# The first unit of a linear-attention and MLP kernel in two halves of 128 tokens

## The chip, the cores and the metric

The kernel runs on 1 core of one Trainium2 chip. The metric is the device time of one execution in microseconds (us), as a median over executions.

The engines are named as in the profile: PE (TensorE, products), PEld (its weight loads), DVE (VectorE), ACT (ScalarE), POOL (GpSimd), SP (SyncE, which issues nearly all transfers). "L445" is line 445 of the kernel.

## The reference

A gated linear attention with a state of 48x48 per head, then an MLP over all 8 heads of a token.

```python
batch, n_heads, seq, head_dim = (4, 8, 768, 48)      # q, k, v, f_logit: float32
...
f = 1.0 / (1.0 + np.exp(-f_logit))
for t in range(S):
    state = f[:, :, t, :, None] * state + np.einsum('bhd,bhe->bhde', k[:, :, t], v[:, :, t])
    y[:, :, t] = np.einsum('bhd,bhde->bhe', q[:, :, t], state)
...
x = np.ascontiguousarray(attn_out.transpose(0, 2, 1, 3)).reshape(B * S, H * D)   # 3072 x 384
h = x @ w_in                                          # 384 x 2048
g = h * (1.0 / (1.0 + np.exp(-1.702 * h)))
return (g @ w_out).astype(np.float32)                 # 2048 x 384
```

The two weights of the MLP are float64, so the kernel also turns 2 x 6.3 MB of 8-byte words into float32.

## The kernel before

**Units.** The 3072 tokens are 12 units of 256, three to a batch entry. In a unit the tokens are two sets of 128, "f = 1" (the first 128, in order) and "f = 0" (the last 128, stored in reverse), each of two chunks of 64. Heads stand in pairs: 128 partitions are two heads of 64 rows, and a tile `X[:, s]` of 128x512 holds one set of q or k for the four pairs.

**Attention of a unit.** `turn` transposes f_logit, k and q by products with the identity (units 0 and 1, L376) and ScalarE writes them to `F` and `X` (L381); later units use VectorE's transposes (L364). `begin_gates` multiplies the gates in pairs, in quarters, and so on (GpSimd, L436). Then six levels, m = 1, 2, 4, 8, 16, 32: `set_aside` copies the keys to `Kc` (ScalarE, L514), `score` makes 16 products (L445), `promote` multiplies keys and queries by the gates of the level (VectorE, L539 for units 0 and 1, one instruction for keys and one for queries, both sets in each), and `evacuate` moves the masked scores to `A` (VectorE L486 and L505, for the last level ScalarE L495). `turn_k` turns the keys back (L618, L619, tile `kn`), the "S" part makes the chunks' sums (L666) and states (L688 to L692) and the products of `A` with v (`add`, L555), and the "W" part adds the products of the queries with the states (L713), copies y to `yT` (L728) and brings it into the MLP's layout `xT` by transfers (`to_x`, L778 and L783): head pairs of 2x48 rows become tiles of 128 rows.

**MLP.** Units 0 and 1 run it plainly: `mlp_h` (L1127, three products per 128 columns of w_in, then GELU by ScalarE, L1131) and `mlp_o` (L1141, one product of 384 columns per 128 rows of w_out and 128 tokens), in four blocks of four 128-wide pieces, whose results are summed (L1191, L1193). Unit 2 uses plain h products and a form of `mlp_o` with fewer products on sums of parts of w_out (L808, L894); units from 3 on also a form of `mlp_h` on sums of parts of w_in (L1033).

**Weights.** They come in 16 pairs, four to a block: two of w_in (ff 0 and 1, ff 2 and 3), then two of w_out. `fetch_weights` issues a pair (768 KB) on SP's queue into one of three buffers `bits`, so pair n can be issued when pair n - 3 is converted. The conversion is an activation on the high words in place (ScalarE, L239), low words times 2^-29 (VectorE, L235), high words shifted (VectorE, L228) and the sum into the weight (VectorE, L238).

**What sets the order.** For TensorE and GpSimd the program's order holds throughout; until `fill_order.close()` (L1383) it holds for all engines. `opening` writes out unit 0 by hand and puts unit 1's transposes between its levels. From unit 1 on, `follow` runs the parts of a unit and, behind each part, a string of steps from `PLAN`: "f" emits the next piece of MLP work from the list `fill` (four or three products), "c" one step of a conversion, "w" a fetch, "p" the beginning of a conversion, "s" a sum of weights, "k" a product that nobody uses (`keep_up`, L116). `HOLES` holds such steps for inside unit 2's levels. The list `fill` has blocks (unit, block) in the order (0,0), (0,1), then (1,0) with (1,1), (0,2) with (1,2), (0,3) with (1,3). An assertion keeps a product behind the conversion of its weights. PSUM for products comes from four banks in turn (`bank`).

Of the kernel before, what the change touches and what calls it, by code (L numbers as in the profile page):

```python
# [23 lines left out]
def kernel(  # L24
# [77 lines left out]
    chosen = []  # L102

    def bank(shape, name, lane=None):

        if lane is None:
            lane = chosen.pop(0) if chosen else next(turns) % 4
        return ps.tile(shape, F32, tag=f"mm{lane}", name=name, bufs=1)
# [11 lines left out]
    nc.scalar.activation(ones, ones, AF.Sigmoid)  # L120
# [22 lines left out]
    nc.gpsimd.memset(by_half[:, :, 1, :, R4 * D - 32:], 0.0)  # L143
# [30 lines left out]
    NGR = NFF // FG  # L174

# [15 lines left out]
    R_BY_ACT = range(0)  # L191
# [18 lines left out]
    def begin_pair(m):  # L210
# [19 lines left out]
        def low():  # L230
            t["r"] = tmp("a", 2).bitcast(I32)
            if m in R_BY_ACT:
                nc.scalar.activation(t["r"], lo.bitcast(U32), AF.Copy, scale=2.0 ** -29)
            else:
                ve.tensor_scalar(t["r"], lo.bitcast(U32), 2.0 ** -29, None, op0=ALU.mult)  # L235
# [4 lines left out]
        if m in R_BY_ACT:  # L240
            low()
        else:
            todo.append(low)
        todo.extend((high, both, None))

    def begin_next():

        if state["begin"] < len(pairs):
            begin_pair(state["begin"])
            state["begin"] += 1  # L250
# [12 lines left out]
    HOLES = {(N_FILL, 0): "ccp", (N_FILL, 1): "cwcc", (N_FILL, 2): "cwp", (N_FILL, 3): "cc", (N_FILL, 4): "cw"}  # L263
# [5 lines left out]
    def load_raw(n, j, engines=(nc.sync,)):  # L269
# [8 lines left out]
        if n < N_FILL:  # L278
            for a in range(NP):
                engine = engines[a * len(engines) // NP]  # L280
                to = by_pair[j][32 * a:32 * (a + 1), :, :R * D]
                if first < 0 and a == 0:

                    for r, rows in ((1, 16), (17, 15)):
                        engine.dma_start(
                            out=to[r:r + rows], in_=span(0, r * R - 1, [[R * D, rows], [S * D, 2], [1, R * D]])
                        )
                    engine.dma_start(out=to[:1, :, D:], in_=span(0, 0, [[R * D, 1], [S * D, 2], [1, (R - 1) * D]]))
                else:
                    engine.dma_start(out=to, in_=span(2 * a, first, [[R * D, 32], [S * D, 2], [1, R * D]]))  # L290
            return
# [46 lines left out]
    def attention(n):  # L338
# [19 lines left out]
        def turn(j, outs, fn=None, pieces=None):  # L358
# [12 lines left out]
            for j0 in pieces or range(0, R, 4):  # L371
# [7 lines left out]
                for f in (1, 0):  # L379
                    at, step = (j0, 1) if f else (HALF - 1 - j0, -1)  # L380
                    nc.scalar.activation(  # L381
                        view(outs(f), at, [[HALF, NP], [R * step, 16], [step, 4]]),
                        pt.rearrange("p j (a f i) -> p f a i j", a=NP, f=2)[:, 1 - f],
                        (AF.Tanh if n > 1 else AF.Sigmoid) if fn else AF.Copy, scale=0.5 if fn and n > 1 else 1.0,
                    )
            if fn and n > 1:
                half_up()
# [264 lines left out]

        @part("S")
# [134 lines left out]
        return (begin_f, begin, begin_k, begin_gates), parts, (open_level, open_evacuate, turn_k), lambda: reverse_v(n)  # L788
# [315 lines left out]
    xTs, halves = {}, []  # L1104

# [7 lines left out]
    def mlp_h(n, ffs, g):  # L1113
        t = {}

        def one(ff, c):
            if c == 0:
                if ff % FG == 0:

                    if not halves:  # L1120
                        new = g_tile(f"g_{n}_{ff}")
                        halves.extend((new[:, :FG], new[:, FG:]))
                        g["tile", ff // HF] = new
                    g[ff // FG] = halves.pop(0)
                t["ph"] = bank([P, U], f"h_{n}_{ff}")
            ph = t["ph"]
            nc.tensor.matmul(  # L1127
                ph, lhsT=w_in[:, ff // 2, c, ff % 2 * P:(ff % 2 + 1) * P], rhs=xTs[n][:, c, :], start=(c == 0), stop=(c == NK - 1)
            )
            if c == NK - 1:  # L1130
                nc.scalar.activation(g[ff // FG][:, ff % FG, :], ph, AF.Gelu_apprx_sigmoid)  # L1131
        return [(NK * U, lambda ff=ff: [one(ff, c) for c in range(NK)], ff // FG * NPC + ff % FG + 1) for ff in ffs]

    def mlp_o(n, ffs, g, done):
# [3 lines left out]
        def one(tt, ff):  # L1138
            if ff == ffs[0]:
                t["po"] = bank([P, DM], f"o_{n}_{tt}_{ff}")  # L1140
# [4 lines left out]
            if ff == ffs[-1]:  # L1145
                done(tt, t["po"])
        return [(DM, lambda tt=tt, ff=ff: one(tt, ff), ff // FG * NPC + FG + 2 + ff % FG // 2 * 2) for tt in range(U // P) for ff in ffs]
# [34 lines left out]
    def mlp_block(n, r):  # L1182
# [13 lines left out]
        return mlp_h(n, ffs, g), mlp_o(n, ffs, g, done)  # L1196
# [10 lines left out]
    def parts_of(n):  # L1207
# [3 lines left out]
        if n and n != N_FILL:  # L1211
            kind, scores = parts[0]
            _, ahead = units[n - 1][1][-1]
# [60 lines left out]
    def follow_steps(steps):  # L1274

        for step in steps:
# [5 lines left out]
            elif step == "p":  # L1282
                begin_next()
            elif step == "w":
                fetch_weights()
# [25 lines left out]
    def opening():  # L1311

        begin_f, begin, begin_k, begin_gates = units[0][0]
        next_f, next_q, next_k, next_gates = units[1][0]
        level, evacuate, turn_k = units[0][2]
        load_raw(0, 0)
        load_raw(0, 2)
        load_raw(0, 1, (nc.scalar,))
        fetch_weights()
        begin_f()  # L1320
        begin_gates()
        begin_k()
        begin()
        load_raw(1, 0)
        load_raw(1, 2)
        load_v(0)
        load_raw(1, 1)
        fetch_weights()
        fetch_weights()
        for l in range(NL):  # L1330
            chosen[:] = [2, 3][l % 2:][:1]
            level(l)
            if l in (2, 3):
                next_f((0, 4)[l - 2:][:1])
            elif l < NL - 1:
                keep_up(1)
            if l == 1:
                begin_pair(0)
                state["begin"] = 1

        nc.scalar.activation(q_end, q_end, AF.Gelu_apprx_sigmoid)
        chosen[:] = [2, 3]
        turn_k(0)
        turn_k(2)
        for l in range(NL - 1):
            evacuate(l)
            if l == 1:
                units[0][3]()
        chosen[:] = [2, 3, 2, 3]
        next_q()  # L1350
        begin_pair(1)
        state["begin"] = 2
        evacuate(NL - 1)
        units[0][1][-2][1]()
        next_gates()
        for _ in range(NOP):
            convert()
        fetch_weights()

    fill = []  # L1360
    opening()
    FIRST = 'k'
    PLAN = {
        3: (
            "fffffffsffsf", "fsffsffsf", "f", "fsfsfsffsfsfsf", "", "ffff", "ff", "ffffffffffffffffsffsf", "fffsf",
        ),
        1: (
            "cccwcccwkkkkk", "kkkcf", "cfccwf", "fcffcwffcffcf", "ffcc", "f", "cwc", "fcc", "ffcf", "pw", "fw", "ff",
            "fffffff",
        ),  # L1370
        2: (
            "ffff", "ffffffff", "fcfcfcwffcfcfcwfffcfcfcff", "sss", "fcfcfcfffffss", "fcfcfcffffffff", "",
            "fffffffffff",
# [3 lines left out]
    fill += mlp_blocks((1, 0), (1, 1)) + mlp_blocks((0, 2), (1, 2)) + mlp_blocks((0, 3), (1, 3))  # L1377
# [4 lines left out]
    assert state["fetch"] == len(pairs)  # L1382
    fill_order.close()  # L1383
    assert state["done"] == 2 * len(pairs) or moe_w_in.dtype == F32
# [49 lines left out]
```

## Time and profile before

| | us |
|---|---|
| median of 3 executions (586.05 to 587.43) | 586.17 |
| the profiled execution, its time | 587.35 |
| its span | 585.4 |
| busy in the span: PE, PEld, DVE, ACT, POOL | 564.4, 514.6, 441.0, 288.8, 142.5 |
| first product of the MLP (L1127) starts | 38.95 |
| first product of unit 1's MLP starts | 69.36 |

TensorE is the busiest engine. A busy TensorE isn't one at its peak, since the ends of products are modelled; the weight loads beside it and the idle products (L116: four at the start and 24 between 13.3 and 38.7 us) tell more. A matrix product in float32 shows as two instructions. The time of an engine's wait matters only where what it then does ends last.

### The profile page before, as it was taken

The page shows a single profiled execution, that of the slowest core. Times are in us where ns is not written, and L with a number is a line of the kernel's source. Part 1 is how long each engine was busy: PE and PEld are TensorE (multiplying, and loading weights), DVE is VectorE, ACT ScalarE, POOL GpSimd, SP SyncE. Part 2 cuts the span into 40 slices and gives each one's busy share as a digit, 9 for nine tenths or more (in the row PEclk, how much of TensorE's full clock was granted, in tenths as well). Part 3 has the DMA queues.
Part 4 walks back from the last instruction along what each step waited for, and adds up shares of the span by engine and source line. Part 5 has one row for each costly group of instructions (what it writes and reads, how often), then busy time and mean ns, then how long its engine had stood idle before and what let it go on. Part 6 is the DMA issues. An engine that isn't in the chain of part 4 may idle for free.

```text
span 585.4 us, 18532 instructions
## 1 busy us (share of the span) xinstructions
PE 564.4 (96%) x7838; PEld 514.6 (88%) x7838; DVE 441.0 (75%) x697; ACT 288.8 (49%) x588; POOL 142.5 (24%) x226
## 2 busy tenths in 40 slices
PE   7899889999999999999999999999999999999997
PEld 6767667676899999999999999999999999999896
DVE  2898877986888786887796897786897786461284
ACT  4755354323543563564563564563563563652440
POOL 4020220614452602402502502502402403103000
PEclk9999999999999999999999999999999999999999
DMA  7869695833352452453542343442451211001000
GB/s 183 197 185 221 172 241 133 234 79 89 100 143 55 126 125 58 116 128 82 131 113 56 103 128 86 126 115 57 120 130 43 64 39 29 29 2 36 19 1 28
DMA packets 86771, 60.34 MB, mean 103 GB/s; under 512 B 33505, under 2 KB 78465, under 8 KB 86689
## 3 DMA queue, kind: packets, MB, share of 16 engines
q1 hardware_dynamic: 86208, 58.57, 40.0%
q8 instruction: 62, 1.02, 0.7%
q10 hardware_dynamic: 481, 0.59, 0.4%
q14 instruction: 20, 0.16, 0.1%
HBM read 45.49 MB, written 8.91 MB: 93 GB/s over the span
## 4 chain that ended last, share of the span: by engine, by line
PE 73%; DVE 10%; DMA 7%; SPq 4%; ACT 3%; issue 2%; ACTq 0%; DVEq 0%
PE h L1033 17%; PE o_Y L894 14%; PE o_Z L894 9%; PE h_y L1033 6%; PE sc L445 6%; PE o_X L894 5%; PE o_W L894 4%; DMA bits<-in_moe_w_in_dram 3%; PE h L1127 3%; PE o L1141 3%; DVE X L364 2%; PE y L713 2%; PE y L555 2%; PE sc L666 2%; DVE X L543 1%
## 5 line engine op out<-in xcount | busy, mean ns | idle before, releaser
L543 DVE TENSOR_TENSOR X<-X,tot 128x1024 f32<-128x1024 f32 x50 | 67.7, 1354 | 44.7 <-PE sc L445 38.4
L514 ACT COPY Kc<-X 128x512 f32<-128x512 f32 x72 | 48.4, 672 | 81.6 <-DVE X L543 61.2
L995 POOL TENSOR_TENSOR E<-xT 128x128 f32<-128x128 f32 (+1 forms) x36 | 16.0, 455 | 229.4 <-DMA xT<-yT 229.4
L1127 PE MATMUL h<-xT,w_in 128*128 128x256 f32 x288 | 65.9, 383 | 2.6 <-DMA xT<-yT 1.8
L1127 PEld LDWEIGHTS h<-xT,w_in 128*128 128x128 f32 x288 | 53.7, 190 | 12.3 <-issue 2.4
L1033 PE MATMUL h<-E,w_in 128*128 128x128 f32 (+1 forms) x476 | 62.8, 277 | 0.5 <-DVE g L1061 0.5
L1033 PEld LDWEIGHTS h<-E,w_in 128*128 128x128 f32 x476 | 57.4, 192 | 1.4 <-issue 0.8
L894 PE MATMUL o_Y<-T,S 128*128 128x192 f32 x320 | 57.7, 329 | 0.0
L1063 ACT ACTIVATE g<-g 128x512 f32<-128x512 f32 (+1 forms) x70 | 40.4, 590 | 27.1 <-DVE g L1061 26.8
L894 PEld LDWEIGHTS o_Y<-T,S 128*128 128x128 f32 x320 | 52.2, 190 | 0.6
L1061 DVE TENSOR_TENSOR g<-g,h 128x512 f32<-128x512 f32 (+1 forms) x58 | 36.1, 637 | 15.3 <-PE h L1033 14.4
L364 DVE STREAM_TRANSPOSE X<-raw 128x512 f32<-128x512 f32 x40 | 42.4, 1115 | 3.1 <-PE y L713 1.8
L1141 PE MATMUL o<-w_out,g 128*128 128x384 f32 x128 | 43.7, 491 | 0.1
L505 DVE COPY_PREDICATED A<-masks,sc 128x256 f32<-128x256 uint32 (+1 forms) x98 | 41.8, 505 | 0.1
L1141 PEld LDWEIGHTS o<-w_out,g 128*128 128x128 f32 x128 | 23.7, 190 | 14.9 <-ACT g L1131 0.4
L728 ACT COPY yT<-y 48x256 f32<-48x256 f32 (+1 forms) x66 | 21.1, 370 | 29.3 <-PE y L713 28.9
L391 POOL TENSOR_SCALAR F<-F 128x1024 f32<-128x1024 f32 x10 | 12.8, 1278 | 87.0 <-ACT F L394 87.0
L1052 ACT ACTIVATE g<-h 128x512 f32<-128x512 f32 (+1 forms) x52 | 28.6, 577 | 9.4 <-PE h L1033 9.0
L445 PE MATMUL sc<-X,Kc 48*64 48x64 f32 x1344 | 28.3, 220 | 3.7 <-ACT Kc L514 2.1
L445 PEld LDWEIGHTS sc<-X,Kc 48*64 48x64 f32 x1344 | 24.1, 134 | 8.0 <-ACT Kc L514 4.4
L894 PE MATMUL o_X<-w_out,g 128*128 128x192 f32 x160 | 29.6, 331 | 0.5 <-ACT o_X L858 0.5
L894 PE MATMUL o_W<-T,g 128*128 128x192 f32 x160 | 29.5, 331 | 0.0
(161 smaller groups left out, 1187.2 us busy)
## 6 DMA issues: line engine op xcount, KB each, us to landing
bits<-in_moe_w_out_dram SPq DMA_DIRECT2D x8, 768.0 KB
raw<-in_f_logit_dram SPq DMA_DIRECT2D x48, 96.0 KB
raw<-in_k_dram SPq DMA_DIRECT2D x48, 96.0 KB
bits<-in_moe_w_in_dram SPq DMA_DIRECT2D x8, 576.0 KB
raw<-in_q_dram SPq DMA_DIRECT2D x44, 96.0 KB
k_tok<-z SPq DMA_DIRECT2D x64, 64.0 KB
kt<-k_tok SPq DMA_DIRECT2D x16, 256.0 KB
out_dram<-osb SPq DMA_DIRECT2D x20, 192.0 KB
```

The lines of the kernel that those rows point to most:

```text
L364: nc.vector.transpose(view(out, at, [[HALF, NP], [step, R4], [R4 * step, 32]]), by_half[:, j, f].rearrange("p a (j d) -> p (a j) d", j=R4) ...
L445: nc.tensor.matmul(t["sc"][h][g * HS:(g + 1) * HS, a, s, :], lhsT=t["Kc", l][rows(h), x:x + HS], rhs=rhs(h, a, g), start=True, stop=True,)
L505: moved = nc.vector.copy_predicated(out=view(A, c * HALF + at, dims), mask=mask.bitcast(U32), data=got)
L514: nc.scalar.copy(c.rearrange("p (n two m) -> p n two m", two=2, m=m), view(X, KF * SLOT, [[2 * m, SLOT // (2 * m)], [(KR - KF) * SLOT + m, ...
L543: nc.vector.tensor_tensor(x, x, y, ALU.mult)
L894: nc.tensor.matmul(t[name], lhsT=lhs(f), rhs=rhs(f), start=(new and i == 0), stop=(i == HF - 1), skip_group_check=True,)
L1033: nc.tensor.matmul(ph[:, t], lhsT=WA[a][:, f // 2, f % 2 * P:(f % 2 + 1) * P], rhs=E[n][b], start=(root and t == 0), stop=not goes_on, ski ...
L1052: nc.scalar.activation(to, ph, AF.Copy, scale=float(sign))
L1061: nc.vector.tensor_tensor(to, to, part, ALU.add if sign > 0 else ALU.subtract)
L1063: nc.scalar.activation(to, to, AF.Gelu_apprx_sigmoid)
L1127: nc.tensor.matmul(ph, lhsT=w_in[:, ff // 2, c, ff % 2 * P:(ff % 2 + 1) * P], rhs=xTs[n][:, c, :], start=(c == 0), stop=(c == NK - 1))
L1141: nc.tensor.matmul(t["po"], lhsT=g[ff // FG][:, ff % FG, tt * P:(tt + 1) * P], rhs=w_out[:, ff, :], start=(ff == ffs[0]), stop=(ff == ffs[ ...
```

## The change

1. **Unit 0 in halves.** A new class `halves` holds unit 0's attention for one set f at a time: `turn` (transposes of 64 tokens' rows by a part of the identity, 64x64), `gates`, `aside` and `aside_q` (keys and queries of one set copied for a level), `promote` (one instruction of 128x256 for keys, one for queries), `score` (16 products of 32 columns), `evacuate`, `turn_k`, `sums`, `state`, `intra`, `inter`, `to_x`. `first_half` takes the place of `opening` and calls them in the order of `OPENING`: "a" levels are those of f = 1, "b" levels those of f = 0, capitals S I W X the first half's sums, products and x, small s i w x the second's, F K Q G unit 1's transposes and gates. The idle products of the opening and of unit 1 are gone.
2. **x by products.** For unit 0, y of a half is copied to `yT` in one instruction and brought into `xT` by products with a selection matrix (kept in w_out's last piece until that is converted) and with parts of the identity, instead of by transfers.
3. **h in halves.** The first block of unit 0 makes its h for 128 tokens at a time: first half's h, then the o products of the first 128 tokens, then the second half's h, then the other o products.
4. **Gates.** Unit 0 and 1 get their gates by tanh and a multiply-add (VectorE or GpSimd) instead of a sigmoid, so one activation table serves all.
5. **Low words by ScalarE.** A step "a" begins a conversion whose low words ScalarE makes (L241 of the new kernel); in the built order nine of the 16 pairs are such.
6. **Loads.** Raw loads of units 0 and 1 go by set, 64 partitions each; SP issues weight pairs 1 and 2 ahead of unit 1's raw loads.
7. **Plan.** `PLAN` and `HOLES` are new, and `fill` has (0,0), (0,1), (0,2), then (1,0), (1,1), (1,2), then (0,3), (1,3). A bank held by an unfinished o product is left out of the turn.

```diff
-    nc.scalar.activation(ones, ones, AF.Sigmoid)
+    nc.scalar.activation(ones, ones, AF.Gelu_apprx_sigmoid)
...
+    select = w_out[:, NFF - 1, :P]
+    nc.gpsimd.tensor_copy(select[:, :D2].rearrange("p (h d) -> p h d", h=2), view(ident, 0, [[HS, 2], [1, D]]))
+    nc.gpsimd.tensor_copy(select[:, D2:].rearrange("p (h d) -> p h d", h=2), view(ident, DR, [[DR, 2], [1, DR // 2]]))
...
-            if m in R_BY_ACT:
+            if by_act:
                 nc.scalar.activation(t["r"], lo.bitcast(U32), AF.Copy, scale=2.0 ** -29)
...
+        class halves:
+            def turn(j, f):
+                rows_ = slice(HS * (1 - f), HS * (2 - f))
+                pt = bank([P, R, HS], f"t_0_{j}_{f}")
+                for jj in range(R):
+                    for h in range(2):
+                        nc.tensor.matmul(
+                            pt[h * HS:(h + 1) * HS, jj, :], lhsT=by_pair[j][rows_, h, jj * D:jj * D + HS],
+                            rhs=ident[rows_, rows_], start=True, stop=True,
+                        )
...
+            def promote(l, f, keys):
+                m, i = LEV[l], ORDER.index(f)
+                w = SLOT // m
+                s, at = ((KF, QF) if f else (KR, QR))[not keys], 0 if keys == f else m
+                x = view(X, s * SLOT + at, [[2 * m, w // 2], [1, m]])
+                y = view(t["tms"][l], i * w + (at == 0), [[2, w // 2], [0, m]])
+                nc.vector.tensor_tensor(x, x, y, ALU.mult)
...
+            def to_x(f):
...
+                nc.scalar.copy(
+                    view(yT[:HS + D], at, [[G, NP], [step * HS, NG], [step, HS]]),
+                    t["py"][:HS + D].rearrange("p g a f t -> p f a g t")[:, f],
+                )
+                pt = bank([P, NK, G], f"x_{f}")
+                for c in range(NK):
+                    nc.tensor.matmul(
+                        pt[:D2, c, :], lhsT=select[:HS + D, :D2], rhs=yT[:HS + D, c, :], start=True, stop=True
+                    )
+                    rest = (ident[:HS + D, :DR], select[:HS + D, D2:], ident[:HS + D, HS + DR // 2:HS + D])[c]
+                    nc.tensor.matmul(pt[D2:, c, :], lhsT=rest, rhs=yT[:HS + D, NK, :], start=True, stop=True)
+                nc.scalar.copy(xTs[n][:, :, (1 - f) * G:(2 - f) * G], pt)
...
+        if (n, r) == (0, 0):
+            h = [mlp_h(n, ffs, g, half) for half in range(2)]
+            return h[0] + o[:FG] + h[1], o[FG:]
...
-    def opening():
+    def first_half():
...
+        def level(l, f):
+            if l == f == 0:
+                reverse_v(0)
+                one.aside(0, 0)
+            one.score(l, f)
+            one.promote(l, f, True)
+            if l + 1 < NL:
+                one.aside(l + 1, f)
+            else:
+                one.evacuate(l, f)
+                one.turn_k(f)
+            one.promote(l, f, False)
+            if l + 1 < NL:
+                one.aside_q(l + 1, f)
+            if l:
+                one.evacuate(l - 1, f)
...
+    OPENING = 'a0 f a1 a2 a3 a4 k q a5 b0 S I W t X b1 b2 b3 F b4 Q b5 s i u K w x G'
     PLAN = {
         3: (
-            "fffffffsffsf", "fsffsffsf", "f", "fsfsfsffsfsfsf", "", "ffff", "ff", "ffffffffffffffffsffsf", "fffsf",
+            "fffffffffffffffsff", "ffssf", "f", "ffffssffffsffffffffff", "f", "", "ff", "fffffffffffffffffff", "fff",
+        ),
+        0: (
+            "", "", "", "p", "cc", "", "", "", "", "c", "", "pc", "", "", "ccw", "wf", "ccfpf", "", "cf", "", "c",
+            "c", "cwc", "c", "", "", "", "acww", "",
         ),
         1: (
-            "cccwcccwkkkkk", "kkkcf", "cfccwf", "fcffcwffcffcf", "ffcc", "f", "cwc", "fcc", "ffcf", "pw", "fw", "ff",
-            "fffffff",
+            "ffccfcfafffc", "ffwcfcw", "ffcffa", "cfaffcfa", "fwcfcffff", "cfcac", "w", "", "cffafww", "cfff", "c",
+            "afcffff", "ff",
         ),
         2: (
-            "ffff", "ffffffff", "fcfcfcwffcfcfcwfffcfcfcff", "sss", "fcfcfcfffffss", "fcfcfcffffffff", "",
-            "fffffffffff",
+            "faff", "fffffpafpffpp", "ccsfffcfffffssffff", "", "fffsffsff", "", "ff", "fffff",
         ),
     }
     fill += mlp_blocks((0, 0)) + mlp_blocks((0, 1))
-    fill += mlp_blocks((1, 0), (1, 1)) + mlp_blocks((0, 2), (1, 2)) + mlp_blocks((0, 3), (1, 3))
+    fill += mlp_blocks((0, 2)) + mlp_blocks((1, 0), (1, 1), (1, 2)) + mlp_blocks((0, 3), (1, 3))
+    first_half()
```

## The prediction

> **What bounds the kernel now.** I read the engines' shares first, then the busy time by stage, TensorE's waits, and the timelines of the opening.
>
> ```profile
> span 585.4 us, 18532 instructions
> ...
> PE   7899889999999999999999999999999999999997
> PEld 6767667676899999999999999999999999999896
> DVE  2898877986888786887796897786897786461284
> ```
>
> Rows of the page: busy tenths in 40 slices. TensorE is full from the third slice on; the weight loads show that its first 39 us and much of the next hundred carry less. The same by stage (columns: PE, PEld, DVE, ACT, POOL busy):
>
> ```profile
> 0.00:38.95 38.95, 31.97 (x660) 25.92 (x661) 25.91 (x56) 22.85 (x52) 10.40 (x30) 1.00 0.71 178
> 38.95:175.40 136.45, 131.68 (x1491) 100.79 (x1490) 115.09 (x165) 60.15 (x124) 40.47 (x34) 1.00 0.65 161
> 175.40:585.40 410.00, 400.75 (x5690) 387.90 (x5689) 300.00 (x478) 205.85 (x412) 91.66 (x163) 1.00 0.30 77
> ```
>
> 38.95 is unit 0's first h product; 175.40 is the end of unit 2's o_W, where the built order of TensorE of both kernels becomes the same to the end. In the second stage TensorE lacks 136.45 - 131.68 = 4.8 us, and its waits (total, times, longest) account for 4.6:
>
> ```profile
> PE h L1127 <- DMA xT<-yT: 1.8, 1, 1.8
> PE sc L445 <- ACT Kc L514: 1.2, 1, 1.2
> PE h L1127 <- ACT g L1131: 0.8, 1, 0.8
> PE sc L445 <- DVE A L505: 0.6, 1, 0.6
> PE sc L666 <- ACT kn L641: 0.2, 1, 0.2
> ```
>
> By starts of products instead of ends I count 5.9 us lost, so 136.4 - 5.9 = 130.5 us of work there. Only two places have time to give: the opening, where TensorE follows a chain and runs idle products (L116) to pass the time, and these 6 us.
>
> ```profile
> 4.72 6.93 PE L376 MATMUL t<-ident,raw 128*64 128x128 f32 x96 [1.05 <-DMA raw<-in_f_logit_dram]
> 12.64 0.70 PE L445 MATMUL sc<-X,Kc 48*64 48x64 f32 x32 [1.00 <-ACT X L381]
> ...
> 31.09 1.04 PE L713 MATMUL y<-X,st 48*48 48x64 f32 x46 [0.23 <-ACT y L677]
> ...
> 37.23 1.88 PE L116 MATMUL idle<-masks,ident 128*128 128x320 f32 x6
> 38.95 1.46 PE L1127 MATMUL h<-xT,w_in 128*128 128x256 f32 x6
> ```
>
> ```profile
> 26.54 0.35 DVE L688 COPY st<-pd 128x192 f32<-128x192 f32 x1
> ...
> 31.54 1.03 DVE L238 CUSTOM_DVE_ANT_0 w_in<-s,a 128x1536 uint16<-128x1536 uint16 x1
> ...
> 34.44 0.55 DVE L235 TENSOR_SCALAR a<-bits 128x768 int32<-128x768 uint32 x1
> ```
>
> ```profile
> 14.88 0.62 ACT L514 COPY Kc<-X 128x512 f32<-128x512 f32 x1 [1.73 <-DVE X L539]
> 15.41 0.95 ACT L239 ACTIVATE bits<-bits 128x768 f32<-128x768 f32 x1
> ```
>
> **The change, step by step**, in us from the span's start; handoffs from these timelines: VectorE to ScalarE 0.1, into or out of TensorE 0.3.
>
> *First half to its first score.* f_logit is two transfers in place of four, so the last issue is at 1.2, not 2.1; with the 2.6 us from issue to first product, 3.8. Its 32 instructions of 64 columns: the first transposes run at half the later pace (0.213 us per two of 128 columns, then 0.107; 96 took 6.93 us, 32 later ones 1.97), so 1.7, and tanh starts at 5.8. Then on ScalarE three moves of 128x512 (0.6 each) and one set-aside: first score 9.2 instead of 12.64.
>
> *Six levels of 128 tokens.* A promotion of 128x256 isn't in the trace; bounds 0.35 (128x192, above) and 0.69 (128x512), taken by columns 0.42, 0.35 behind another. Copies of 128x256 on ScalarE 0.40. Two promotions and an evacuation (0.37) are 1.1 a level, so is the ring promote, hand over, set aside, hand over; before, 1.64 (12.64 to 20.84 in five). In the ring stand also tanh of the other half (0.6), pair 0's L239 (0.93), two conversions (1.1; 2.3 while GpSimd works, as 1.32 for L235 at 29.29 shows) and 1.2 for k and q: last score done at 18.0.
>
> *Its x.* A by ScalarE 0.75, kn 0.6, the other half's first set-aside 0.45, its score 0.8, sums 0.9, conversion and state 1.0, inter 0.7, pair 1's L239, which stands ahead of yT in ScalarE's queue, 0.9, yT 0.9, twelve products 1.6, xT 0.8: 9.4 with little overlap, so unit 0's first h at 27 instead of 38.95. The products replace six yT copies and five transfers (32.3 to 38.9) and cost TensorE 12 x 0.109 = 1.3 per half (128-column rows of L618). The table load of 1.28 us at 20.54 is gone; it is in this sum.
>
> *Second half.* From 27 TensorE has four half h (0.65 each), four scores (0.5), unit 1's six transposes (5.9), tkn and sums (2.5), 13 us. VectorE has ten promotions (3.5), four evacuations (1.5), four state steps (1.6) and pairs 2 to 4 (0.55 + 0.55 + 0.96 each, 6.2), 12.8. ScalarE has eight set-asides (2.9), three L239 (2.8), twelve pieces of unit 1 (3.6), four GELUs (1.1), A and kn (1.35) and single copies (1.8), 13.5. Each queue is in order and waits for the other two, so 13.5 is the least; if half of what the fullest queue does stood alone it would be 20. I take 15.6, nearer the lower end since the level rings interleave with conversions that wait for nobody: y of the second half is copied at 42.6, and only there is TensorE full. Before, unit 0 was whole at 38.95, so the early start is worth 2.6 us of h, while the whole unit comes later.
>
> *Weights.* SP now issues pairs 1 and 2 ahead of unit 1's raw loads, pair 3 behind them and behind pair 0's conversion. Ahead of pair 3's end stand raw of two units (2.36 MB), v (0.39) and four pairs (3.15), 5.9 MB from 2 us on: it lands at 26.5 at the page's best slice (241 GB/s) and at 34 at the mean of 0 to 40 (183); ScalarE wants it at 30. I take no wait; the bound is 4 us, in front of the fourth level's copies.
>
> *After it.* Work left: 130.5 - 2.6 + 1.3 (two scores of unit 1 that the kernel before had behind it at 38.95) = 129.2, and x 0.3 + 1.3.
>
> *The fill.* Unit 0's third block now goes ahead of unit 1. Behind unit 1's inter stand 16 o instructions (5.2 us) where 12 were (3.9 and the wait of 1.8), so that wait shrinks to 0.5, but pair 14 is fetched in front of xT on SP's queue (768 KB, 3.2 us at 241 GB/s, a part of it before yT is copied): 1.2. kn of unit 1 stands behind pair 11's two ScalarE conversions: 0.7. Further waits for Kc behind conversions: 1.6 (bounds 0 and 5). Sum 3.5, where 5.9 was. The chain over memory to unit 3's kn covers as before: 18.9 us from score to sums, and 19.3 of products stand there now.
>
> *At nothing:* nine low words leave VectorE (9 x 0.55 = 5.0) for ScalarE (about 0.93 each by L239, 8.4); TensorE waits for neither conversion now, and ScalarE is busy 60 of 136 us. If that cover is gone, each delays by 0.93 a GELU that frees a bank. The half_up of unit 1 on GpSimd (1.3 to 1.6) ends 6 us before VectorE needs F. GpSimd's added clears and copies end before F is there. SP's raw loads are as many bytes as before.
>
> **Sum**: 42.6 + 0.3 + 1.3 + 129.2 + 3.5 = 176.9 against 175.4, +1.5 us. The profiled execution, 587.35 (span 585.4 and 1.95 around it), becomes 588.9; it is 1.2 above the median of 586.17, on which I forecast **587.7**, own range 585.7 to 589.7.
>
> **Rivals.** *Faster:* the first half is there 1 us sooner and the second takes ScalarE's bare 13.5 (y at 39.5) and one us of waits is left: 171.3, -4.1, 582.1; with the waits of the forecast it decides from y at 41.1 (175.4 - 129.2 - 1.6 - 3.5) downward. For it: VectorE has 9 us less to convert after 39 us (nine low words, and pairs 3 and 4 already done); against: the queues are 82 to 87% full there even at 15.6, and serial. *ScalarE's queue:* L239 of pairs 7 to 12 stand ahead of the Kc copies and GELUs; their transfers are issued only when three pairs earlier is done and follow unit 2's raw loads (704 KB each, 3.6 us at the 195 GB/s of 100 to 120), landing by my count 0.3 to 3 us before use; the point is whether pair 9 is there at 60. If four come 1.2 late, +5 more: 592.7. For it: ScalarE waited 7.5 us for w_in before. *The clock:* before, L116 kept TensorE busy; now nothing does. If it falls back to the half pace of its first transposes in 9 to 43, the second half's 13 us become 26: +11 more, 598. For it: the scores fill some 40% of 9 to 18; against: the longest gap I count is 1.6 us, and after the gap of 1.05 us at 27.8 the products here kept their pace. [...] *The change gives nothing of what it says:* that ScalarE's low words alone move the time; here 0.
>
> **Chances.** Forecast 0.45 (0.25 within 0.3%, or 1.8 us, which is about what can be told from no change; 0.2 slower), faster rival 0.30, ScalarE's queue 0.15, the clock 0.10. Faster 0.30, same 0.25, slower 0.45. The range goes from somewhat beyond the faster case, 580.5, to beyond the queue's, 594.
>
> **What would show it.** First h near 27; yT of the second half near 42.6; unit 1's h near 84; o_W's end near 177. I am wrong if the second half's y is there by 40, if TensorE's waits after it pass 6 us, or if transposes of unit 1 run at half pace.

## Result: 603.3 us, and the profile after

The changed kernel takes **603.30 us** (median of 4 runs, 601.83 to 604.75) where the kernel before takes 586.80 beside it: a ratio of **1.0274** (95% interval 1.0259 to 1.0290). The forecast was 587.7, the range 580.5 to 594. The profiled execution took 601.83, of which 600.0 are its span. Executions of one kernel lie apart here, those of one with added idle products by up to 21 us (595.28 to 616.23); so with a median stands, where a trace is read, the time of its own execution, and the ratios leave out executions more than 1.5% above the fastest of their kernel.

From the page, busy tenths in 40 slices of 15 us:

```profile
span 600.0 us, 19214 instructions
...
PE   7898999999999999999999999999999999999997
PEld 6776776868689899999999999999999999999897
DVE  3657879786797977788787798787797786462284
```

TensorE looks as full as before, VectorE emptier in the second and third slice (6, 5 for 8, 9). By stage (PE, PEld, DVE, ACT, POOL busy, clock, DMA share, GB/s), cut at unit 0's first h, at the first x product of the second half, and at the first o_X product behind o_W (175.22 in the trace before):

```profile
0.00:36.67 36.67, 28.84 (x549) 24.36 (x549) 17.10 (x43) 14.73 (x32) 9.28 (x37) 1.00 0.56 154
36.67:56.07 19.40, 16.62 (x353) 14.91 (x349) 13.34 (x27) 11.84 (x32) 3.15 (x3) 1.00 0.74 170
56.07:190.28 134.21, 132.45 (x1565) 101.72 (x1566) 107.80 (x152) 64.59 (x132) 39.13 (x37) 1.00 0.59 145
190.28:600.00 409.72, 401.17 (x5691) 388.13 (x5690) 300.48 (x479) 205.85 (x413) 94.56 (x165) 1.00 0.30 77
```

The third stage is what the forecast said: 134.2 us, against 1.3 + 129.2 + 3.5 = 134.0. The last is the kernel before's. All the loss is in the opening: the x products of the second half begin at 56.07, not at 42.9 (y at 42.6, copied in 0.3). TensorE's timeline there (start, length, work, idle time before it):

```profile
5.65 6.02 PE L672 MATMUL t<-ident,raw 64*64 64x64 f32 x94 [0.55 <-DMA raw<-in_f_logit_dram]
12.45 1.08 PE L730 MATMUL sc<-X,Kc 48*64 48x32 f32 x32 [0.78 <-ACT X L678]
...
36.67 1.65 PE L1310 MATMUL h<-xT,w_in 128*128 128x128 f32 x6
38.24 1.08 PE L730 MATMUL sc<-Qc,Kc 48*64 48x32 f32 x32
39.25 2.85 PE L1310 MATMUL h<-xT,w_in 128*128 128x128 f32 x12
42.03 0.67 PE L730 MATMUL sc<-Qc,Kc 48*64 48x32 f32 x32
42.63 1.97 PE L387 MATMUL t<-ident,raw 128*64 128x128 f32 x32
44.53 0.71 PE L1310 MATMUL h<-xT,w_in 128*128 128x128 f32 x4
```

The same 32 score products take 1.08 us up to 38.24 and 0.67 from 42.03 on; six h instructions take 1.65 at 36.67 (0.94 at 64.30), the x products of the first half 3.7 us (31.94 to 35.66), those of the second 2.17. **TensorE works at half pace up to about 41.5 us.** The clock column reads 1.00 all the while. TensorE's waits from the second half's x products on (total, times, longest), and from ScalarE's queue a half-width copy and its wait for the fourth weight pair (start, length, work, idle time before):

```profile
PE x L822 <- ACT yT L816: 1.1, 1, 1.1
PE h_None L1310 <- DMA xT<-yT: 1.0, 1, 1.0
PE sc L845 <- ACT kn L630: 0.7, 1, 0.7
```

```profile
12.20 0.41 ACT L700 COPY Kc<-X 128x256 f32<-128x256 f32 x1
...
44.50 0.91 ACT L247 ACTIVATE bits<-bits 128x768 f32<-128x768 f32 x1 [3.29 <-DMA bits<-in_moe_w_out_dram]
```

The first of these waits ends at 56.07, with the x products; behind it only 1.7 us are left (3.5 forecast). The half-width copies take 0.41, near the 0.40 they were given. The fourth pair is late: 3.3 us, where I took none.

### The profile page after: what moved, and what is told of

The parts are those of the page before. It is cut to its first block, busy times and chain, and to the rows that moved or that the text cites. A ratio compares the mean times of both kernels' runs of the same rounds, so it can differ in the third digit from the quotient of the medians.

```text
span 600.0 us, 19214 instructions
## 1 busy us (share of the span) xinstructions
PE 579.1 (97%) x8150; PEld 529.1 (88%) x8150; DVE 438.7 (73%) x699; ACT 297.0 (50%) x608; POOL 146.1 (24%) x240
## 3 DMA queue, kind: packets, MB, share of 16 engines
q8 instruction: 64, 1.05, 0.7%
## 4 chain that ended last, share of the span: by engine, by line
PE 83%; DVE 5%; ACT 4%; DMA 3%; POOL 2%; issue 2%; SPq 1%; ACTq 0%; DVEq 0%; POOLq 0%
PE h L1212 15%; PE o_Y L1073 12%; PE h_None L1310 10%; PE o_Z L1073 8%; PE o L1324 6%; PE sc L456 6%; PE h_y L1212 6%; PE o_X L1073 4%; PE o_W L1073 4%; PE y L892 2%; PE y L566 2%; PE sc L845 2%; PE t L672 2%; DVE X L554 1%; PE sc L730 1%
## 5 line engine op out<-in xcount | busy, mean ns | idle before, releaser
L525 ACT COPY Kc<-X 128x512 f32<-128x512 f32 x66 | 44.2, 670 | 81.3 <-DVE X L554 66.9
L1174 POOL TENSOR_TENSOR E<-xT 128x128 f32<-128x128 f32 (+1 forms) x36 | 17.9, 508 | 229.3 <-DMA xT<-yT 229.3
L1310 PE MATMUL h_None<-xT,w_in 128*128 128x256 f32 x264 | 60.1, 383 | 1.0 <-DMA xT<-yT 1.0
L1310 PEld LDWEIGHTS h_None<-xT,w_in 128*128 128x128 f32 x264 | 49.3, 190 | 9.3 <-issue 1.6
L1242 ACT ACTIVATE g<-g 128x512 f32<-128x512 f32 (+1 forms) x70 | 40.4, 590 | 26.5 <-DVE g L1240 26.4
L516 DVE COPY_PREDICATED A<-masks,sc 128x256 f32<-128x256 uint32 x88 | 38.5, 512 | 0.1
L907 ACT COPY yT<-y 48x256 f32<-48x256 f32 (+1 forms) x60 | 19.2, 369 | 26.8 <-PE y L892 26.4
L1212 PE MATMUL h<-E,N_c 128*128 128x128 f32 (+1 forms) x212 | 27.4, 276 | 0.8 <-POOL E L1174 0.8
L1073 PE MATMUL o_Z<-w_out,g 128*128 128x192 f32 x160 | 28.2, 327 | 0.0
```

The lines of the kernel that those rows point to most:

```text
L516: moved = nc.vector.copy_predicated(out=view(A, c * HALF + at, dims), mask=mask.bitcast(U32), data=got)
L525: nc.scalar.copy(c.rearrange("p (n two m) -> p n two m", two=2, m=m), view(X, KF * SLOT, [[2 * m, SLOT // (2 * m)], [(KR - KF) * SLOT + m, ...
L1073: nc.tensor.matmul(t[name], lhsT=lhs(f), rhs=rhs(f), start=(new and i == 0), stop=(i == HF - 1), skip_group_check=True,)
L1212: nc.tensor.matmul(ph[:, t], lhsT=WA[a][:, f // 2, f % 2 * P:(f % 2 + 1) * P], rhs=E[n][b], start=(root and t == 0), stop=not goes_on, ski ...
L1242: nc.scalar.activation(to, to, AF.Gelu_apprx_sigmoid)
L1310: nc.tensor.matmul(ph, lhsT=w_in[:, ff // 2, c, ff % 2 * P:(ff % 2 + 1) * P], rhs=xTs[n][:, c, cs], start=(c == 0), stop=(c == NK - 1))
```

## The experiments

**Idle products in the changed kernel: is it the pace?** Three runs. The first makes the idle products at the start ten instead of four (counted, as in the profile, by instructions, two to a product); the second puts one pair behind steps of the opening; the third does both.

```diff
-    keep_up(2, 192, (flat_A[:, :P], flat_A[:, :192]))
+    keep_up(5, 192, (flat_A[:, :P], flat_A[:, :192]))
...
+    # behind a0 to a5, b0, S, I, W, b1, b2, b3 (second and third run)
+    keep_up(1, 192, (ident, masks[:, :192]))
```

> The changed kernel with ten idle products of 128x192 on the whole array in place of four before f_logit is there (about 2.0 to 6.1 us), nothing else. Theory A (the pace): the changed kernel loses its time because TensorE stays at half pace to 41.5 us, and it stays there because products on a 64x64 part of the array do not bring it up; products on the whole array do, so the first transposes run at 0.053 us an instruction or less in place of 0.064 with scores of 32 at 0.67 in place of 1.08, at least up to the first gap; if the pace then holds, y of the second half is there near 49 in place of 56.0 and the time is 595 to 598. If small products do not hold it either, it falls back within 10 us and the time stays at 602 to 603. Theory B (the chain): the opening is set by VectorE, ScalarE and the transfers; the pace changes nothing and the time stays within 1 us of 603, scores of 0.67 or not.

> The changed kernel with one idle product of 128x192 on the whole array (two instructions) behind each of thirteen steps of the opening's levels, start unchanged. Theory A: TensorE comes to full pace somewhere in 13 to 25 us and keeps it; x products of the first half at 1.6 us in all in place of 3.7, scores 0.67; y of the second half between 48 and 52, time 594 to 599. Theory B: the idle products only stand in the way, 0.3 to 0.6 us each where the chain waits for a score, and the time is 603 to 608.

> Both edits: ten idle products at the start and one behind each of thirteen steps. Theory A: full pace from 6 to 42 us as in the kernel before, y of the second half near 47, time 591 to 596, the lowest of the three. Theory B: as with the levels' idle products alone, 603 to 608.

Measured: 603.26 (1.0264, 1.0242 to 1.0287), 608.69 (1.0358, 1.0317 to 1.0399) and 610.11 (1.0371, 1.0328 to 1.0414). By time alone theory B, that the pace changes nothing, would stand; the traces say otherwise. In the first run the pace did come up at about 7 us (the 32 transposes at 7.92 take 1.46, between 1.97 at half and 1.15 at full pace) and was lost by 12.3 (1.08 a score), behind waits of 0.5 for k and q; its clock row reads 0.50 from 12 to 44 (0.966 over the execution). In the second it did not come before 49, though PE busy (the first number behind the length) reads, in four stretches:

```profile
17.00:24.00 7.00, 7.00 (x124) 5.35 (x118) 5.58 (x13) 4.06 (x10) 2.81 (x7) 1.00 0.63 153
24.00:31.00 7.00, 6.65 (x108) 5.71 (x110) 1.00 (x4) 2.82 (x6) 0.00 (x0) 1.00 0.63 194
31.00:38.00 7.00, 7.00 (x119) 5.27 (x120) 3.98 (x9) 1.86 (x5) 0.00 (x0) 1.00 0.66 167
38.00:45.00 7.00, 7.00 (x53) 4.65 (x54) 2.40 (x6) 1.65 (x4) 0.00 (x0) 1.00 0.60 166
```

and in its timeline, in the midst of that:

```profile
18.52 1.08 PE L730 MATMUL sc<-Qc,Kc 48*64 48x32 f32 x32
19.54 1.01 PE L121 MATMUL idle<-masks,ident 128*128 128x192 f32 x2
20.47 1.08 PE L730 MATMUL sc<-Qc,Kc 48*64 48x32 f32 x32
```

TensorE is busy in 27.65 of 28 us and stays at half pace, so gaps are not what keeps it there. In the first stretch about half of the time is idle products on the whole array, over all four 9.9 of 28 us; most of the rest is scores, transposes and sums on 48x64 or 64x64 parts of it. The idle products did not wake TensorE and stood in the way at 1.01 a pair.

**The kernel before without its idle products, and with small ones.** In the first all of its `keep_up` products but the four at the start are left out; in the second they stay, as many and as long, on a quarter of the array.

```diff
-            nc.tensor.matmul(pt, lhsT=lhs, rhs=rhs, start=True, stop=True)
+            nc.tensor.matmul(pt[:HS], lhsT=ident[:HS, :HS], rhs=masks[:HS], start=True, stop=True)
```

> The kernel before without any of its idle products but the first four (all of those on masks and ident, in 13 to 39 us, are left out). Theory A, strong form (only whole-array work counts and small gaps matter): TensorE falls back to half pace after the opening transposes, scores take 1.1 in place of 0.69, unit 0's first h comes 1 to 3 us later than 38.95 and starts slowly, time 588 to 592. Theory A, weak form (once up, scores and transposes hold it): same time as before, 586 to 587.5. Theory B: 585 to 587, the idle products being only ballast.

> The kernel before with all of its idle products but the first four on a 64x64 part of the array, as many and as long (64 rows and 64 columns of the identity against 320 columns). If TensorE's being busy is what holds the pace: same time as before, 586.5 to 588, scores 0.69 in 14 to 20. If it is the part of the array that works: the pace falls in 14 to 21 or behind 33 us as in the run without any idle products, scores or h at half pace there (1.1 and 0.33 an instruction of h), time 590 to 593.

Measured: 591.75 without (1.0066, 1.0044 to 1.0088) and 591.90 with small ones (1.0074, 1.0056 to 1.0092): 4.0 and 4.1 us behind the kernel before of their own comparisons (587.72, 587.76). TensorE with small ones:

```profile
13.86 0.70 PE L449 MATMUL sc<-X,Kc 48*64 48x64 f32 x32 [1.02 <-ACT X L385]
14.38 0.70 PE L118 MATMUL idle<-masks,ident 64*64 64x320 f32 x2
...
17.15 1.13 PE L449 MATMUL sc<-X,Kc 48*64 48x64 f32 x32 [0.41 <-DVE X L543]
18.21 1.97 PE L380 MATMUL t<-ident,raw 128*64 128x128 f32 x16
...
41.33 2.93 PE L1131 MATMUL h<-xT,w_in 128*128 128x256 f32 x6
```

The same falls in both: 1.11 to 1.13 a score at 17 and h at half pace from 41 (2.93 for six, 1.46 before). So the idle products of the kernel before are no ballast. With small ones TensorE is also a little less busy (2.42 us of the 3.29 from the first score to the third, 2.87 of 3.30 in the kernel before), so this run alone doesn't part the two; together with the 28 us above it points to **how much of the array works, not that TensorE is busy**.

**The raw loads.** In 2 to 9 us the changed kernel moved 88 GB/s with 0.26 of its DMA engines' time busy; the kernel before 241 with 0.84, some 56 of it on ScalarE's queue. A packet of 1536 bytes takes 65 ns in both (median), so fewer engines share the work: 0.26 of 16 is 4.2, and 0.84 is 13.4. The change writes a transfer's source as 4 pairs by 16 rows, the kernel before as 32 rows by 2 heads. My estimate from that 4.2 is that a source with 4 slowest keeps a transfer on 4 engines; three runs try other cuts. The first run cuts by rows at half the size (48 KB), the second adds idle products up to W, the third gives the kernel before the changed kernel's cut.

```diff
-                        in_=span(2 * a0 + h, token, [[2 * S * D, NP - a0], [R * D, 16], [1, R * D]]),
+                        in_=span(2 * a, token, [[R * D, 16], [S * D, 2], [1, R * D]]),
```

> The changed kernel with its raw loads of units 0 and 1 cut another way: a transfer is one pair of heads, 16 rows by 2 heads (48 KB, rows slowest in the source), where it was one head of all four pairs (96 KB, the four pairs slowest in the source); the first q half goes on ScalarE's queue as in the kernel before. Same bytes, more transfers. Theory C (transfers): while raw loads are under way the changed kernel moves about 100 GB/s with 0.27 of the 16 DMA engines' time busy, where before moved 207 to 261 with 0.7 to 0.9, at the same 63 to 65 ns a packet: a source whose slowest dimension is 4 keeps a transfer on 4 engines. Cut by rows, 4 to 9 us should show above 200 GB/s, the first score come at 9.5 to 10.5 in place of 12.45, the wait of 3.3 us for the fourth weight pair go, y of the second half be there at 50 to 52.5 in place of 56.0, and the time be 596 to 600. Theory A (the pace alone): the first score comes earlier by at most 1 us and the time stays at 602 to 604.

> The same loads, with idle products on the whole array as well: eight of 128x192 at the start, two behind each of the first three turns, and two of 128x256 or 128x192 behind each of a0 to a5, b0, I and W of the opening. Theories A and C together: with the data there early TensorE has no long wait before the first score, comes to full pace at about 5 us and keeps it: scores 0.67, x products of the first half 1.7 in all; y of the second half at 45 to 48, time 590 to 595. C alone: no better than without the idle products, 596 to 602.

> The kernel before with its raw loads of units 0 and 1 cut as in the changed kernel: one head of all four pairs per transfer (2 transfers of 192 KB in place of 4 of 96 KB, the four pairs slowest in the source), else as before. Theory C: its opening loads run at about 100 GB/s too, the transposes of unit 0 wait for them, the first score comes 3 to 5 us later than 12.64, and the time is 591 to 597. Without C: 586 to 588.

Measured: 603.66 (1.0278, 1.0249 to 1.0306), 602.04 (1.0234, 1.0202 to 1.0267), 605.24 (1.0305, 1.0277 to 1.0334). The last has the cut alone and moved 84 GB/s in 2 to 9 us. Its waits of TensorE in 0 to 45 us (total, times, longest):

```profile
PE t L374 <- DMA raw<-in_f_logit_dram: 6.3, 2, 4.1
PE t L374 <- DMA raw<-in_k_dram: 4.7, 2, 4.5
PE t L374 <- DMA raw<-in_q_dram: 2.2, 1, 2.2
```

Its first score comes at 26.55 instead of 12.64; that it pays more than the changed kernel I put down to its needing whole units, which no run shows. In the changed kernel the first run gained only 0.8 us at the first score (11.61), as SP issues a transfer of 48 KB in 0.45 us (128 GB/s in 4 to 8), and nothing at the end. The second held the pace up to 26 us: first score 10.57, last of the first half done at 21.0 (24.9 in the changed kernel), then a wait of 1.75 us and half pace to 43.

**Loads by rows at full size.** Rows become the slowest dimension in place, with the copies out of the transposes reading their columns in that order; q's first half on ScalarE's queue. The second and third run add idle products, the third the most (two of 320 columns behind a0, a1, a2, a5 and W).

```diff
+    in_=span(h, token + R * skip, [[R * D, 16 - skip], [2 * S * D, NP], [1, R * D]]),
...
-    pt.rearrange("p j (a i) -> p a i j", a=NP),
+    pt.rearrange("p j (i a) -> p a i j", a=NP),
```

> The changed kernel with the same number of raw transfers of the same size (one head of all four pairs, 96 KB), but rows slowest in the source: partition 4*i+a holds the rows i of pair a, where it was 16*a+i, and the copies out of the transposes read their columns in that order; the first q half on ScalarE's queue. No idle products. The run with 48 KB transfers moved only 128 GB/s in 4 to 8 us, as SP issues one in 0.45 us, so it did not test what full transfers are worth. Theory C: 180 GB/s and more in 3 to 8 us; f, k and q of the first half there by 7; the first score at 11 to 11.6, as the transposes at half pace (1.97 us a turn) then set it; the wait for the fourth weight pair falls from 3.3 to below 1.5 us; y of the second half at 53 to 55, time 599 to 602. Theory A (half pace decides the rest): no more than that.

> The same loads, with idle products on the whole array: eight of 128x192 at the start, two behind each of the first three turns, two behind a0 to a5 (128x256) and behind b0, S, I, W, b1 and b2 (128x192). In the run with idle products to W alone the pace held to 26 us and was lost behind a wait of 1.75 us; from 28 to 44 TensorE was then full at half pace and set the time of the second half's levels. Theory A: with the pace held to 44 us those 16 us become 8 to 10: y of the second half at 45 to 48, time 589 to 594. Rival (the ring over VectorE and ScalarE sets the second half, as the prediction had it): y not before 51, time 597 to 601, at whatever pace.

> The rows-outer loads with more idle products on the whole array: two of 128x320 behind a0, a1, a2, a5 and W, two of 128x256 behind a3, a4, b0, I, b1 and b2, two of 128x192 behind the second f, S and b3, and those ahead of the first score as in the run before. In the two runs with idle products the pace was lost at 16 us in one and at 26 in the other, at much the same order of work, and their times lie as far apart as 600 to 611. If the pace holds to 44 here: scores 0.67 throughout, first half's last score done at 21 to 22, first h at 31 to 33, y of the second half at 47 to 50, time 591 to 596. What is then left of the loss (4 to 8 us) is not the pace. If it is lost again on the way: 598 to 606, with a spread of several us. If the pace doesn't matter to the time (the ring over VectorE and ScalarE): above 600 although the scores take 0.67.

Measured: 605.61 (1.0285, 1.0248 to 1.0321), 608.11 (1.0261, 1.0209 to 1.0312), 601.91 (1.0192, 1.0144 to 1.0240). The first moved 164 GB/s in 2 to 9 and had its first score at 10.76 (1.7 sooner), and no wait for the fourth pair, yet no better time. TensorE stood still at 22 us:

```profile
PE t L670 <- issue: 2.7, 1, 2.7
```

"issue" is a wait that no semaphore explains. And in its trace the pace, up at 44.5, fell once more at 58:

```profile
57.66 0.41 PE L824 MATMUL x<-yT,ident 112*32 112x128 f32 x2
58.00 0.46 PE L820 MATMUL x<-yT,w_out 112*96 112x128 f32 x2
58.39 0.64 PE L824 MATMUL x<-yT,w_out 112*32 112x128 f32 x2
```

Its clock row reads 0.53 from 58 to 65; the runs with ten idle products at the start and with 48 KB transfers have the same fall (0.51 and 0.55; 1.13 and 1.14 for 32 scores at 59.02 and 59.53, where the changed kernel takes 0.70 at 58.24). In the second run the pace held to 16 us and came back at 33; the x products began at 54.66. In the third the pace held from 5 us on, was lost at 22 behind another such wait (1.35), and came back by 33. Here the clock column does show it:

```profile
4.00:20.00 16.00, 15.10 (x341) 11.09 (x340) 9.23 (x24) 7.67 (x17) 5.76 (x15) 1.00 0.97 230
20.00:32.00 12.00, 11.29 (x180) 8.12 (x182) 4.37 (x11) 4.10 (x10) 0.00 (x0) 0.59 0.59 163
32.00:53.76 21.76, 19.72 (x416) 16.25 (x412) 14.42 (x31) 13.72 (x35) 2.81 (x3) 0.99 0.58 134
```

From its first h to the x products are 17.1 us at full pace, where the changed kernel took 19.4:

```profile
36.69 0.83 PE L1308 MATMUL h<-xT,w_in 128*128 128x128 f32 x6
...
53.76 0.46 PE L820 MATMUL x<-yT,w_out 112*96 112x128 f32 x2 [1.10 <-ACT yT L814]
```

By the spacing of starts 1.1 of these are idle products, which leaves 16.0; in the second run it is 17.05 with 0.4 of them. Its six executions lie between 595.28 and 616.23: two near 596, two near 616, all four with a mean granted clock of 1.00. No trace shows one of these.

**The stall.** In four runs such a wait ended 1.4 to 1.55 us after a packet of 16 KB of instructions had landed (the profile's "instruction" queue, 64 packets and 1.05 MB in the changed kernel), while weight pairs 1 and 2 filled the queues. Both runs fetch these pairs later, the first with the most idle products, the second with none.

```diff
         load_v(0)
-        fetch_weights()
-        fetch_weights()
...
+        # one fetch_weights() behind step k, one behind b0
```

> The run with the most idle products, with weight pairs 1 and 2 fetched later (behind the k turn and b0 of the opening, in place of ahead of it). In four runs TensorE stood still for 1.3 to 2.7 us in 20 to 26 us for no semaphore, and resumed 1.4 to 1.55 us after a packet of 16 KB of instructions had landed, with the transfers of pairs 1 and 2 in the queues (272 to 316 GB/s). Theory D: the instruction load stands behind these transfers; fetched later, it lands in time, that wait is below 0.5 us, the pace holds through to 44 us, y of the second half at 47 to 50, time 592 to 597. If the wait stays, it is not these transfers, and the time is 596 to 604.

> The changed kernel with rows-outer loads and no idle products, with weight pairs 1 and 2 fetched later, else as in the run with these loads that stood still for 2.73 us at 22. Theory D: that wait below 0.5 us, last score of the first half done at 23 in place of 26.4, first h at 35 in place of 38.2, time 600 to 603, two to three less than with the early fetch (605.6), at half pace to 42 as before. If the wait stays: 604 to 606.

Measured: 609.59 median, with executions from 596.12 to 610.83, too far apart for a ratio; and 600.99 (1.0231, 1.0204 to 1.0258). In the second the stall is gone, the first half's last score is done at 23.0 (26.4 with the early fetch), first h at 35.28 (38.15), the second half's x products at 54.17 (57.27). The stall is worth these 3.1 us; the profiled executions differ by 6.2 (599.63 and 605.87), since behind that point only the one with the early fetch has the second fall. That the packet of instructions waited behind the weights remains argued: in the four traces it took 1.1 to 1.35 us to land, and 1.31 in the trace without a stall. In the first run the trace (an execution of 610.53) has TensorE busy without a gap from 4.9 to 41 and at half pace up to 39. Up to 12 us its TensorE has the same instructions as the run with the most idle products, whose pace was up at 5. The 32 transposes at 4.88 in that run and in this one:

```profile
4.88 1.23 PE L670 MATMUL t<-ident,raw 64*64 64x64 f32 x32
```

```profile
4.88 1.97 PE L670 MATMUL t<-ident,raw 64*64 64x64 f32 x32
```

So after the same first instructions the pace came at 5 us in one execution and at 39 in another; how the execution of 596 went no trace shows.

**The x products alone**, in the kernel before, instead of its five transfers; the second run clears the y tiles earlier and leaves out the idle products behind.

> The kernel before with one part of the change alone: unit 0's x by products with parts of the identity (two token halves of six products of 128 columns, 112 rows, two copies out), in place of the five transfers; three of its idle products behind the second score and two of those behind the third are left out, as the new products stand there. The y copies stay six; they end at 34.3 in the kernel before, the transfers land at 38.9. If the x products are worth what the prediction took (1.3 a half and a copy of 0.5): first h at 36.5 to 37.5 in place of 38.95, time 584 to 586, 1 to 2.4 below before. Rival: TensorE only waits later, for conversions on VectorE (busy 7.5 of 8 us there), and for unit 1: 586.5 to 588. If the fewer idle products let the pace fall: 589 to 592.

> The kernel before with unit 0's x by products once more, cleaned: in the run before, the products stood 1.69 us behind a clear on GpSimd, the pace fell there and twelve products took 0.68 each. Now the y tiles are cleared at the start, and the products stand right behind the first score of unit 1, without idle products behind them. If the part is worth what the prediction took: products from 33.5 to 36.2 at 0.43 each, first h at 36.5 to 37.5 in place of 38.95, 584.5 to 586.5. Rival (VectorE's conversions and unit 1 take it back): 587 to 588.5. If the pace falls all the same in the wait ahead of them: 590 to 596.

Measured: 597.03 (1.0159, 1.0138 to 1.0181) and 592.13 (1.0083, 1.0060 to 1.0106). In the first the x products waited 1.69 us for a clear by GpSimd and fell to half pace (from 0.41 to 0.64 for two). The second's timeline:

```profile
34.60 0.43 PE L748 MATMUL x<-yT,w_out 112*96 112x128 f32 x2 [0.88 <-POOL tot L441]
...
38.58 0.41 PE L750 MATMUL x<-yT,ident 112*32 112x128 f32 x2
...
39.56 1.56 PE L1151 MATMUL h<-xT,w_in 128*128 128x256 f32 x6
43.25 0.69 PE L450 MATMUL sc<-X,Kc 48*64 48x64 f32 x32 [2.13 <-ACT Kc L519]
```

At full pace the products take 4.3 us for both halves, not 2.6; h comes at 39.56, not sooner than 38.95, and a wait of 2.1 for Kc follows. Part of the rest is the pace again (1.13 a score at 16.63). No version tried beats the kernel before.

## Why the prediction was wrong

- **What fell is one assumption of the opening: that TensorE is at full pace behind the first transposes** ("the first transposes run at half the later pace"). It was taken from the kernel before, whose transposes use 128 rows. By the spacing of their starts (0.213 us per two, then 0.109) the pace comes up 3.0 us into them there, and within 6 us in all six traces that have them (5.8 in the one without idle products). Those of the change use 64 rows. That 5.4 us of them without a gap stay at half pace (4.60 to 9.98 in the run with loads by rows) would alone not tell them apart; but in all five traces with four idle products at the start the pace came only behind 40 us, when h products on the whole array had begun.
- The rival **The clock** (0.10) had the cause and nearly the price (598). It lay low for two wrong reasons. It spoke of a fall, and there was none, since the pace was never up; and I weighed it by the gaps ("the longest gap I count is 1.6 us"), while 27.65 busy us of 28 did not bring it up. Nor does a fall want a long gap: in the kernel before without idle products the pace fell at 17 us, among gaps of 0.90 to 0.99 (the gap at 27.8 that I quoted for it is 0.96, not 1.05). That the price came near is in part luck: it laid all 11 us on the second half, where the pace cost about 3; the rest fell on pieces that it left out. How long TensorE was busy does not tell when the pace comes: it came 3.0 to 5.8 us into the transposes of 128 rows, and not within the 28 us above.
- **First half to its first score**: 12.45, not 9.2. "SP's raw loads are as many bytes as before" was true and beside the point: with 4.2 of 16 engines busy (0.26) they land late. Loads by rows bring it to 10.53 (the late-fetch run), full pace as well to 10.09; the other 0.9 was mis-sized.
- **Six levels**: 12.4 us, not 8.8. With the pace held 10.4 (10.57 to 21.0), so 2.0 are the pace. The ring over VectorE and ScalarE does not feel it: VectorE's promotions take 8.2 us there (11.36 to 19.57) and 8.3 in the changed kernel (13.66 to 21.94). I summed it too short, by at most 1.6, as idle products stand in the 10.4, though its pieces were right (0.42 a promotion, 0.40 a copy).
- **Its x**: 11.8, not 9.0. The twelve instructions of its six products take 3.7 at half pace, 2.17 at full; I gave them 1.6, so 0.6 of it is a size taken from 128-column rows of another shape.
- **Second half**: 19.4, not 15.9 (27 to 42.9). At full pace it is about 16 (16.0 and 16.6 without the idle products of two runs): this sum was right, and about 3 are the pace.
- Those four are +3.2, +3.6, +2.8 and +3.5, the 13.2 by which the opening ended late. Some 2 us of them are the loads, up to 3 mis-sized terms, and the rest, about 8, the pace; the split of the third rests on durations, as no trace has it at full pace throughout. That is an account of durations and not a time won back: with pace and loads both mended for most of the opening the median is still 601.91 and the best execution 595.28. Of the 15.6 us that the forecast missed, 12.9 are in the profiled execution (601.83 for 588.9); the other 2.7 come from adding to a median what was read from one execution.
- **Weights**: "I take no wait; the bound is 4 us": 3.3 for ScalarE. TensorE's wait behind it, for Qc at 46.22, is 0.75; by rows both are gone.
- **After it and the fill**: right in the sum, 134.2 for 134.0, partly by luck. The x products cost 0.9 more than given and the waits 1.8 less; the other 1.1 I can't name.

## What to carry to other kernels

When work is cut into smaller pieces, ask for each engine what the smaller piece does to its pace and not only how long it is: transposes of 64 rows and scores of 32 columns did not by themselves wake TensorE here, however dense (5.4 us of such transposes without a gap stayed at half pace). Read a transfer's source as its dimensions in order, not only as its bytes (88 GB/s with 4 pairs slowest, 164 with 16 rows). And read the pace by the spacing of one kind of product over time, before and after, since neither the busy shares nor the clock row showed it.

## What the runs showed of the hardware

- Products on a 48x64 or 64x64 part of the array did not raise TensorE's pace (1.08 for 32 scores up to 38.24 in the changed kernel, 0.67 from 42.03), and small idle products did not hold it (4.1 us lost with them, 4.0 with none). Some 10 us of whole-array products in 28 busy us did not raise it either. Which measure decides, rows, columns or both, isn't settled.
- After the same instructions up to 12 us, full pace came at 5 us in one execution and at 39 in another. One kernel's executions lay between 595 and 616 us.
- The clock column reads 1.00 for a half pace that stands from the start (up to 41.5 us in the changed kernel, over the first 3.0 us of transposes in the kernel before), and 0.59 (20 to 32 us of the run with the most idle products) where the pace fell after it had been up.
- Loads with a source whose slowest dimension is 4 moved 84 and 88 GB/s in 2 to 9 us (the kernel before cut so, the changed kernel), with 16 rows slowest 164, with 32 rows 241; a packet of 1536 bytes took 65 ns in the changed kernel and in the kernel before.
- TensorE stood for 1.3 to 2.7 us with no semaphore to explain it, until 1.4 to 1.55 us after 16 KB of instructions had landed; with weight pairs 1 and 2 fetched later the wait was gone in both runs.
